# A one-element GpSimd add that reads the last prepared weight, ahead of GpSimd's first weight sums, and a newly searched list of steps, in a chunked-attention and gated feed-forward kernel

## The chip, the cores and the metric

The kernel runs on one core of a Trainium2 chip. The core's engines are TensorE (PE, matmuls; PEld is its weight load), VectorE (DVE), ScalarE (ACT), GpSimd (POOL) and SyncE (SP), which here only issues DMA transfers, one after the other in its program's order. Each engine works through its own instructions in order and waits on semaphores for what others make. The metric is the device time of one execution in microseconds, lower is better.

## The reference

Attention in chunks of 64 rows, without a sum across chunks, and after it a feed-forward layer on all tokens. Both matrices of the layer come as 64-bit floats (in the kernel: pairs of 32-bit words).

```python
scores = scale * q_c @ k_c.T          # q, k, v: (8, 8, 576, 64), chunks of 64
attn = exp(scores - max); attn /= (sum(attn) + 1e-9)
x = (attn @ v_c) laid out as (4608 tokens, 512)
h = x @ w_in                          # 512 x 2048
g = h * sigmoid(1.702 * h)
out = g @ w_out                       # 2048 x 512
```

## The kernel before

Tokens are worked in 9 blocks of 512 (four tiles of 128), and the 2048 hidden columns in 16 slices of 128. A group is one block with one slice; group g of the first three blocks is block g // 16, slice g % 16. For each group PE makes the slice of h (steps `h0_g` and `h_g`, six matmuls of 512 columns each; for groups 0 and 1 it is cut into halves, `hh_0_0`, `h_0_0`, `hh_0`, `h_0` and so on), ACT makes the activation and its rounded high part (`gh_g`), DVE the low part (`gl_g`), and PE adds into the four output tiles (`o_g_0` to `o_g_3`, three matmuls each). Every product is three matmuls on a high and a low part, so both weights and activations are split.

The weights of slice j are loaded by SP (`raw_j`: two transfers of 512 KB, w_in's and w_out's part, L365 and L370), and made into high and low parts by ACT (`wsc_j` L374, `wlow_j` L381, `wh_j` L410) and DVE (`wshift_j` L387, `wj_j` L394, `w_j` L413). DVE's three use one of three buffers called `wtmp`. PE needs `w_j` for `h0_j`.

Attention runs beside it: `q_u`, `k_u`, `v_u` are loads of the first four tiles; `rows0_4` and `rows1_4` load q and k of tiles 4 and 5 (two transfers of 256 KB each, L470). PE transposes those (`tp0_4`, `tp1_4`, L1259), ACT and DVE copy them (`tq0_4`, `tk0_4`), and `s_4` makes the scores. For later pairs of tiles (`s_6`, `s_8`, ...) DVE transposes (`tq0_8`, `tq1_8`, L1277; the attention weights by L1342, `et0_6` to `et_6`) and POOL divides (`n_6`, `n_8`, L1323).

From block 3 on pairs of blocks are multiplied with sums of blocks (seven products P1 to P7 in place of eight). For that POOL adds up parts of each pair of weight slices p: `pa0_p` and `pa_p` (L699, tile `whole`), then four sums (`psum_p`, L706 to L709, tile `sums`); these tiles too are `wtmp` buffers. ACT and DVE split them, SP writes them to a DRAM tile `seven` (`pout`, `pouts`), and later loads the pieces for each product (`ld0_s_p` to `ld6_s_p`, L807 and L809) into six buffers, used in turn.

`ORDER`, a list of 2,693 step names, sets in which order the steps are written to the program, and so the order on every engine and on SP's queue. `Plan.emit` asserts that each step's `need` names stand ahead of it in the list. A `need` is no wait on the chip by itself: the waits follow from the tiles that an instruction reads, writes or takes over.

```python
        plan.add(POOL, 1.3, rank, lambda: whole(0), need=[w0, f"w_{NF - 1}"], make=e("pa0"), take=["tmp"])
```

So in the list `pa0_p` stands behind `w_15`, while `whole(0)` reads only the weights of slice 2p and takes over one `wtmp` buffer.

Of the kernel before, what the change touches and what calls it, by code (L numbers as in the profile page):

```python
# [8 lines left out]
F32 = mybir.dt.float32  # L9
# [5 lines left out]
ALU = mybir.AluOpType  # L15
AX = mybir.AxisListType

PE, ACT, DVE, POOL, DMA = "pe", "act", "dve", "pool", "dma"
# [216 lines left out]
def tile_chunk_attention_ffn(  # L235
# [9 lines left out]
    nc = tc.nc  # L245
# [4 lines left out]
    P = 128  # L250
# [3 lines left out]
    NF = DF // P  # L254
# [1381 lines left out]
    def gelu_table():  # L1636
        z = const.tile([P, P], F32, tag="gelu", name="gelu")
        nc.scalar.activation(z[:, :1], ident[:, :1], AF.Gelu_apprx_sigmoid)
# [55 lines left out]
```

## Time and profile before

| | |
|---|---|
| median of 3 runs | 821.38 us (819.9 to 821.66) |
| the profiled execution | 821.13 us, of which span 819.4 us |
| PE busy | 807.3 us (99%), 6038 matmuls |
| DVE, ACT, POOL busy | 586.2, 383.5, 91.5 us |
| DMA | 131 MB, mean 160 GB/s |

The span runs from the first to the last instruction of the program; times in the rows below are microseconds from its start. Busy time of PE is the union of matmuls whose ends are modelled and overlap, so that a stretch can be fully busy by this count while successive matmuls start 0.23 us apart.

### The profile page before, as it was taken

How to read it: one execution, taken by the hardware profiler on the slowest of the kernel's cores; microseconds unless marked ns; L12 is line 12 of the kernel's file. 1: busy time of each engine (PE TensorE's matmuls, PEld its weight loads, DVE VectorE, ACT ScalarE, POOL GpSimd, SP SyncE). 2: the span in 40 equal slices, each digit the busy share in tenths (PEclk: the TensorE clock that was granted, in tenths of full speed). 3: DMA queues.
4: the chain of work that ended last, by engine and by line, in shares of the span. 5: the costliest groups of instructions: out<-in, count | busy, mean ns of one | idle time of the engine just before them, and what ended most of it. 6: DMA issues, size and time to landing. Idle time of an engine off the chain costs nothing.

```text
span 819.4 us, 15635 instructions
## 1 busy us (share of the span) xinstructions
PE 807.3 (99%) x6038; PEld 680.4 (83%) x6038; DVE 586.2 (72%) x865; ACT 383.5 (47%) x603; POOL 91.5 (11%) x82
## 2 busy tenths in 40 slices
PE   7899999999999999999999999999999999999998
PEld 6788878888888888888888888888888888889998
DVE  5788976356475879885698898776887454569852
ACT  5899824244355536423554352422565311267430
POOL 1000170000063661000001010000000000000000
PEclk9999999999999999999999999999999999999999
DMA  9998645353266677767666437686633047673433
GB/s 242 282 297 244 167 129 123 88 128 72 57 182 174 158 199 207 186 173 219 171 172 167 104 92 193 180 211 198 164 104 116 1 130 213 194 207 118 142 92 103
DMA packets 244010, 131.08 MB, mean 160 GB/s; under 512 B 187104, under 2 KB 211680, under 8 KB 243936
## 3 DMA queue, kind: packets, MB, share of 16 engines
q1 hardware_dynamic: 243936, 130.08, 58.6%
q8 instruction: 48, 0.79, 0.4%
q14 instruction: 26, 0.21, 0.1%
HBM read 97.52 MB, written 32.51 MB: 159 GB/s over the span
## 4 chain that ended last, share of the span: by engine, by line
PE 88%; DVE 4%; SPq 3%; ACT 2%; DMA 2%; issue 1%; DVEq 0%; ACTq 0%
PE po L1553 12%; PE po L1555 12%; PE po L1554 12%; PE hp L820 9%; PE hp L822 9%; PE hp L821 9%; PE hp L1515 4%; PE hp L1513 4%; PE hp L1514 4%; SPq L470 2%; PE s L1293 2%; PE x L1367 2%; DMA w<-seven 1%; DVE wtmp L394 1%; PE acc_X L1069 1%; PE acc_X L1068 1%
## 5 line engine op out<-in xcount | busy, mean ns | idle before, releaser
L1553 PE MATMUL po<-w,g_l 128*128 128x512 f32 x448 | 176.8, 395 | 0.6 <-DVE g_l L1543 0.5
L1555 PE MATMUL po<-w,g_h 128*128 128x512 f32 x448 | 174.5, 390 | 0.0
L1554 PE MATMUL po<-w,g_h 128*128 128x512 f32 x448 | 174.5, 389 | 0.0
L1553 PEld LDWEIGHTS po<-w,g_l 128*128 128x128 f32 x448 | 84.1, 188 | 20.1 <-DVE g_l L1543 1.9
L1555 PEld LDWEIGHTS po<-w,g_h 128*128 128x128 f32 x448 | 84.1, 188 | 17.7
L1554 PEld LDWEIGHTS po<-w,g_h 128*128 128x128 f32 x448 | 84.1, 188 | 16.8
L820 PE MATMUL hp<-w,w 128*128 128x512 f32 x224 | 87.6, 391 | 0.3 <-DMA w<-seven 0.2
L1342 DVE STREAM_TRANSPOSE eT<-e 32x512 f32<-32x512 f32 x120 | 84.2, 702 | 4.4 <-POOL e L1323 2.4
L822 PE MATMUL hp<-w,w 128*128 128x512 f32 x224 | 87.2, 389 | 0.0
L821 PE MATMUL hp<-w,w 128*128 128x512 f32 x224 | 87.1, 389 | 0.0
L1323 POOL TENSOR_TENSOR e<-e,r 128x1024 f32<-128x1024 f32 x16 | 31.2, 1953 | 437.8 <-DVE r L1320 365.0
L1513 PE MATMUL hp<-x_l,w 128*128 128x512 f32 x184 | 72.0, 391 | 0.0
L1515 PE MATMUL hp<-x_h,w 128*128 128x512 f32 x184 | 71.6, 389 | 0.0
L1514 PE MATMUL hp<-x_h,w 128*128 128x512 f32 x184 | 71.6, 389 | 0.0
L1543 DVE TENSOR_TENSOR g_l<-hp,g_h 128x512 fp32r<-128x512 f32 (+1 forms) x50 | 33.2, 664 | 51.9 <-ACT g_h L1538 51.8
L1537 ACT ACTIVATE hp<-hp 128x512 f32<-128x512 f32 (+1 forms) x50 | 28.4, 569 | 66.5 <-PE hp L1515 57.3
L820 PEld LDWEIGHTS hp<-w,w 128*128 128x128 f32 x224 | 42.0, 188 | 10.5 <-issue 1.1
L822 PEld LDWEIGHTS hp<-w,w 128*128 128x128 f32 x224 | 42.1, 188 | 8.8
L821 PEld LDWEIGHTS hp<-w,w 128*128 128x128 f32 x224 | 42.1, 188 | 8.6
L820 PE MATMUL hp<-w,pieces 128*128 128x512 f32 x112 | 43.8, 391 | 0.0
L822 PE MATMUL hp<-w,pieces 128*128 128x512 f32 x112 | 43.6, 389 | 0.0
L821 PE MATMUL hp<-w,pieces 128*128 128x512 f32 x112 | 43.6, 389 | 0.0
(237 smaller groups left out, 1558.6 us busy)
## 6 DMA issues: line engine op xcount, KB each, us to landing
w<-seven SPq DMA_DIRECT2D x112, 256.0 KB, 3.3
pieces<-seven SPq DMA_DIRECT2D x56, 256.0 KB, 3.4
seven<-w SPq DMA_DIRECT2D x24, 512.0 KB, 3.8
raw<-in_moe_w_in_dram SPq DMA_DIRECT2D x16, 512.0 KB, 5.9
raw<-in_moe_w_out_dram SPq DMA_DIRECT2D x16, 512.0 KB, 6.3
four<-four_w SPq DMA_DIRECT2D x32, 256.0 KB, 3.2
raw<-in_q_dram SPq DMA_DIRECT2D x208, 32.0 KB, 2.4
raw<-in_k_dram SPq DMA_DIRECT2D x208, 32.0 KB, 2.2
```

The costliest lines, as they stand in the source:

```text
L820: nc.tensor.matmul(hp, w[:, 0, c], xl[:, c], start=c == 0, stop=False)
L821: nc.tensor.matmul(hp, w[:, 0, c], xh[:, c], start=False, stop=False)
L822: nc.tensor.matmul(hp, w[:, 1, c], xh[:, c], start=False, stop=c == 1)
L1323: nc.gpsimd.tensor_tensor(st["e"], st["e"], bc(st["r"]), op=ALU.mult)
L1342: nc.vector.transpose(st["et"][po : po + 32, :, 32 * a : 32 * a + 32], st["e"][pi : pi + 32, :, 32 * b : 32 * b + 32],)
L1513: nc.tensor.matmul(hp, wh, xl, start=cc == 0, stop=False)
L1514: nc.tensor.matmul(hp, wh, xh, start=False, stop=False)
L1515: nc.tensor.matmul(hp, wl, xh, start=False, stop=cc == NCC - 1)
L1543: nc.vector.tensor_tensor(gl[:, c], hp, gh[:, c].bitcast(F32), op=ALU.subtract)
L1553: nc.tensor.matmul(po, gl[:, c], w[:, 0, :], start=first, stop=False)
L1554: nc.tensor.matmul(po, gh[:, c], w[:, 0, :], start=False, stop=False)
L1555: nc.tensor.matmul(po, gh[:, c], w[:, 1, :], start=False, stop=last)
```

## The change

A step `gate` is added on POOL: it adds one element of the last slice's low weight part to itself, into a tile that nobody reads. `pa0_p` now needs `gate` in the list in place of `w_15`; on POOL `gate` stands ahead of the first `pa0`. The list is another one from its first line on: it has the same names and `gate`.

```diff
-        plan.add(POOL, 1.3, rank, lambda: whole(0), need=[w0, f"w_{NF - 1}"], make=e("pa0"), take=["tmp"])
+        plan.add(POOL, 1.3, rank, lambda: whole(0), need=[w0, "gate"], make=e("pa0"), take=["tmp"])
...
+    def gate():
+        t = const.tile([P, 1], F32, tag="gate", name="gate")
+        w = wt[NF - 1][:, 1, 1, :1].bitcast(F32)
+        nc.gpsimd.tensor_tensor(t, w, w, op=ALU.add)
...
+    plan.add(POOL, 0.12, -80, gate, need=[f"w_{NF - 1}"], make="gate")
...
-    "o_85_0 tlo0_5 d5_1_3 thi1_5 tout0_5 P4_1_3 ld5_1_4 P1_1_4 d6_1_3 h_1_3_two ld3_1_4 tlo1_5 v0_30 gl_86 P2_1_4 "
...
+    "ld3_1_4 d3_1_3 tout_4 o_85_3 ta_5 o_84_1 tsum_5 o_85_0 gh_86 P3_1_3 d4_1_3 thi0_5 ld4_1_4 o_85_1 tlo0_5 P4_1_3 "
```

**The start, SP's queue** (`first_b` are the `v` loads, `rows_4` the loads `rows0_4` and `rows1_4`, `raw_j` the weights), before and then after, from `raw_1` on:

```order
L365 DMA raw_1_237<-in_moe_w_in_dram 128x4x128
L370 DMA raw_1_237<-in_moe_w_out_dram 128x512
L470 DMA rows_4_260<-in_q_dram 128x8x64
L470 DMA rows_4_260<-in_k_dram 128x8x64
L470 DMA first_b_3_245<-in_v_dram 128x8x64
L470 DMA first_b_2_314<-in_v_dram 128x8x64
L365 DMA raw_2_368<-in_moe_w_in_dram 128x4x128
L370 DMA raw_2_368<-in_moe_w_out_dram 128x512
L365 DMA raw_3_385<-in_moe_w_in_dram 128x4x128
```

```order
L365 DMA raw_1_234<-in_moe_w_in_dram 128x4x128
L370 DMA raw_1_234<-in_moe_w_out_dram 128x512
L470 DMA first_b_2_259<-in_v_dram 128x8x64
L470 DMA first_b_3_242<-in_v_dram 128x8x64
L365 DMA raw_2_312<-in_moe_w_in_dram 128x4x128
L370 DMA raw_2_312<-in_moe_w_out_dram 128x512
L470 DMA rows_4_356<-in_q_dram 128x8x64
L470 DMA rows_4_356<-in_k_dram 128x8x64
L365 DMA raw_3_391<-in_moe_w_in_dram 128x4x128
```

The two transfers of `rows0_4` moved from ahead of `raw_2` to behind it; what stands ahead of `raw_3` is the same.

**The start, PE** (`hp_0_1` is the second half of group 0, `hp_1_0` the first of group 1, `qkTp_4_0` is `tp0_4`, `po_0_1` is `o_0_1`), before and after, from the end of `o_0_0` on:

```order
L1555 MATMUL po_0_0_437<-w_0_289,g_h_0_375 128x512
L1553 MATMUL po_0_1_444<-w_0_289,g_l_0_376 128x512
...
L1526 MATMUL hp_0_1_454<-x_h_0_84,w_0_289 128x256 x4
L1526 MATMUL hp_1_0_461<-x_h_0_84,w_1_448 128x256 x4
L1528 MATMUL hp_0_1_454<-x_l_0_85,w_0_289 128x256
...
L1259 MATMUL qkTp_4_0_478<-ident_73,rows_4_260 128x128 x8
L1528 MATMUL hp_1_0_461<-x_l_0_85,w_1_448 128x256
```

```order
L1555 MATMUL po_0_0_435<-w_0_310,g_h_0_382 128x512
L1526 MATMUL hp_0_1_445<-x_h_0_84,w_0_310 128x256 x4
L1259 MATMUL qkTp_4_0_453<-ident_73,rows_4_356 128x128 x8
L1528 MATMUL hp_0_1_445<-x_l_0_85,w_0_310 128x256
...
L1526 MATMUL hp_1_0_479<-x_h_0_84,w_1_442 128x256 x4
L1553 MATMUL po_0_1_485<-w_0_310,g_l_0_383 128x512
...
L1528 MATMUL hp_1_0_479<-x_l_0_85,w_1_442 128x256
```

`tp0_4` moved ahead of `h_0`, `hh_1_0` and `o_0_1`; further on, two of the four `o_1` steps moved ahead of `h0_2`, and the steps up to the first `o_2` are the same set in both.

**The last weights, DVE** (around `g_l_12` and the last three `w_j`), before and after:

```order
L394 ISA wtmp_14_1150<-raw_14_911,wtmp_14_1150 128x2048
L413 TENSOR_TENSOR w_13_1174<-wtmp_13_1140,w_13_1174 128x2x512
L1342 STREAM_TRANSPOSE eT_6_1101<-e_6_1019 32x16x32 x2
L413 TENSOR_TENSOR w_14_1206<-wtmp_14_1150,w_14_1206 128x2x512
L387 TENSOR_SCALAR wtmp_15_1241<-raw_15_1067 128x1024
L1543 TENSOR_TENSOR g_l_12_1224<-hp_12_1186,g_h_12_1223 128x512
L394 ISA wtmp_15_1241<-raw_15_1067,wtmp_15_1241 128x2048
L1342 STREAM_TRANSPOSE eT_6_1101<-e_6_1019 32x16x32 x2
L1277 STREAM_TRANSPOSE qkT_8_1266<-raw_8_965 128x1024 x2
L1543 TENSOR_TENSOR g_l_13_1263<-hp_13_1227,g_h_13_1262 128x512
L413 TENSOR_TENSOR w_15_1253<-wtmp_15_1241,w_15_1253 128x2x512
```

```order
L413 TENSOR_TENSOR w_13_1182<-wtmp_13_1142,w_13_1182 128x2x512
L394 ISA wtmp_15_1184<-raw_15_928,wtmp_15_1184 128x2048
L1342 STREAM_TRANSPOSE eT_6_1128<-e_6_1016 32x16x32 x2
L413 TENSOR_TENSOR w_15_1216<-wtmp_15_1184,w_15_1216 128x2x512
L1543 TENSOR_TENSOR g_l_12_1223<-hp_12_1164,g_h_12_1222 128x512
L413 TENSOR_TENSOR w_14_1236<-wtmp_14_1112,w_14_1236 128x2x512
L1277 STREAM_TRANSPOSE qkT_8_1262<-raw_8_1002 128x1024
L1543 TENSOR_TENSOR g_l_13_1265<-hp_13_1207,g_h_13_1264 128x512
L1342 STREAM_TRANSPOSE eT_6_1128<-e_6_1016 32x16x32 x2
L1277 STREAM_TRANSPOSE qkT_8_1262<-raw_8_1002 128x1024
L1342 STREAM_TRANSPOSE eT_6_1128<-e_6_1016 32x16x32 x2
```

`w_15` came ahead of `g_l_12` and of `w_14`, `w_14` behind `g_l_12`; four of the eight transposes of tile pair 6 and one of pair 8's two now stand behind `g_l_13`.

**The last weights, POOL**, before and after, from `n_6` on:

```order
L1323 TENSOR_TENSOR e_6_1019<-e_6_1019,r_6_1061 128x1024
L699 TENSOR_TENSOR whole_2_1301<-w_4_664 128x512
L699 TENSOR_TENSOR whole_2_1301<-w_5_716 128x512
L699 TENSOR_TENSOR whole_0_1383<-w_0_289 128x512
L699 TENSOR_TENSOR whole_0_1383<-w_1_448 128x512
```

```order
L1323 TENSOR_TENSOR e_6_1016<-e_6_1016,r_6_1074 128x1024
L1639 TENSOR_TENSOR gate_1240<-w_15_1216 128x1
L699 TENSOR_TENSOR whole_2_1242<-w_4_660 128x512
L699 TENSOR_TENSOR whole_2_1242<-w_5_712 128x512
L699 TENSOR_TENSOR whole_0_1275<-w_0_310 128x512
L699 TENSOR_TENSOR whole_0_1275<-w_1_442 128x512
```

The gate stands between `n_6` and the first sums; behind them the order is `psum_2`, `psum_0`, one or both of pair 1, `n_8` in both.

## Rows read from the trace of the kernel before

**Rows 1.** The page's first lines: the span, and busy time, share and instructions of each engine.
```profile
span 819.4 us, 15635 instructions
PE 807.3 (99%) x6038; PEld 680.4 (83%) x6038; DVE 586.2 (72%) x865; ACT 383.5 (47%) x603; POOL 91.5 (11%) x82
```

**Rows 2.** Busy time of each engine in three stretches (start and end, length; then busy us and instructions; granted clock, DMA share, GB/s).
```profile
28.00:48.00 20.00, 18.35 (x163) 15.65 (x164) 17.03 (x24) 18.41 (x25) 0.00 (x0) 1.00 0.99 308
48.00:102.00 54.00, 53.87 (x359) 44.06 (x358) 48.75 (x53) 47.61 (x58) 3.81 (x2) 1.00 0.86 227
102.00:114.00 12.00, 11.49 (x50) 8.88 (x49) 11.85 (x13) 5.40 (x9) 6.45 (x4) 1.00 0.36 121
```

**Rows 3.** What PE waited for from 48 us to the end: us in total, times, longest.
```profile
PE po L1553 <- DVE g_l L1543: 0.5, 2, 0.3
PE hp L820 <- DMA w<-seven: 0.2, 1, 0.2
```

**Rows 4.** The chain that ended last, in order of time, from the transfer of `raw_2`'s second half to the first `o_2` (start, us, what).
```profile
23.82 6.60 DMA raw<-in_moe_w_out_dram
...
48.59 0.50 PE po L1553
```

**Rows 5.** ACT's instructions in order of time, 28 to 48 us: `wh_1`, `wsc_2`, `wsc_3`, `tq1_4`, the second half of `gh_2` (start, us; in brackets idle time before it and what ended it).
```profile
28.61 1.06 ACT L410 ACTIVATE w<-wtmp 128x1024 fp32r<-128x1024 f32 x1
30.50 1.17 ACT L374 ACTIVATE raw<-raw 128x1024 f32<-128x1024 f32 x1 [0.83 <-DMA raw<-in_moe_w_out_dram]
...
33.77 1.17 ACT L374 ACTIVATE raw<-raw 128x1024 f32<-128x1024 f32 x1
...
38.19 0.60 ACT L1266 ACTIVATE qkT<-qkTp 128x512 f32<-128x512 f32 x1 [0.57 <-DVE qkT L1269]
...
46.75 0.60 ACT L1538 ACTIVATE g_h<-hp 128x512 fp32r<-128x512 f32 x1
```

**Rows 6.** SP's issues of the k part of `rows0_4`, of `raw_3`'s second half and of the k part of `rows1_4`, and for each of them the us from issue to landing.
```profile
17.36 0.94 SPq L470 DMA_DIRECT2D rows<-in_k_dram  x1
24.84 0.50 SPq L370 DMA_DIRECT2D raw<-in_moe_w_out_dram  x1
26.16 2.70 SPq L470 DMA_DIRECT2D rows<-in_k_dram  x1
...
rows<-in_k_dram SPq DMA_DIRECT2D x1, 256.0 KB, 6.2
raw<-in_moe_w_out_dram SPq DMA_DIRECT2D x1, 512.0 KB, 8.8
rows<-in_k_dram SPq DMA_DIRECT2D x1, 256.0 KB, 9.0
```

**Rows 7.** PE's matmuls in order of time around the start of the attention of tiles 4 and 5: `o_0_1`, `hh_0` with `hh_1_0`, `tp0_4`, `h_1_0`, `hh_1`, `s_4`.
```profile
28.66 0.40 PE L1553 MATMUL po<-w,g_l 128*128 128x512 f32 x1
...
29.35 1.11 PE L1526 MATMUL hp<-x_h,w 128*128 128x256 f32 x8
...
31.25 1.03 PE L1259 MATMUL qkTp<-ident,rows 128*128 128x128 f32 x8
32.04 0.36 PE L1528 MATMUL hp<-x_l,w 128*128 128x256 f32 x1
...
33.91 0.73 PE L1526 MATMUL hp<-x_h,w 128*128 128x256 f32 x4 [0.68 <-DVE g_l L1543]
...
38.84 1.16 PE L1293 MATMUL s<-qkT 64*64 64x64 f32 x64 [0.97 <-ACT qkT L1266]
```

**Rows 8.** DVE's instructions in order of time: `w_6`, and `w_14`, `gl_12`, `wj_15`, `gl_13`.
```profile
61.73 1.23 DVE L413 TENSOR_TENSOR w<-wtmp,w 128x1024 fp32r<-128x1024 f32 x1
...
103.53 2.23 DVE L413 TENSOR_TENSOR w<-wtmp,w 128x1024 fp32r<-128x1024 f32 x1
...
106.28 0.68 DVE L1543 TENSOR_TENSOR g_l<-hp,g_h 128x512 fp32r<-128x512 f32 x1
106.88 1.70 DVE L394 CUSTOM_DVE_ANT_0 wtmp<-raw,wtmp 128x2048 uint16<-128x2048 uint16 x1
...
112.37 0.65 DVE L1543 TENSOR_TENSOR g_l<-hp,g_h 128x512 fp32r<-128x512 f32 x1
```

**Rows 9.** POOL's instructions in order of time: `pa0_2` with `pa_2`, `pa0_0` with `pa_0`, and `n_8`.
```profile
102.13 2.55 POOL L699 TENSOR_TENSOR whole<-w 128x512 f32<-128x512 f32 x2 [13.39 <-DVE w L413]
105.84 3.90 POOL L699 TENSOR_TENSOR whole<-w 128x512 f32<-128x512 f32 x2 [1.16 <-DVE w L413]
...
133.47 1.90 POOL L1323 TENSOR_TENSOR e<-e,r 128x1024 f32<-128x1024 f32 x1 [10.60 <-ACT hp L1537]
```

**Rows 10.** PE's matmuls in order of time: the first of `h0_6`, of `o_12_3` and of `o_13_3`.
```profile
63.23 0.39 PE L1513 MATMUL hp<-x_l,w 128*128 128x512 f32 x1
...
107.02 0.50 PE L1553 MATMUL po<-w,g_l 128*128 128x512 f32 x1 [0.19 <-DVE g_l L1543]
...
113.08 0.50 PE L1553 MATMUL po<-w,g_l 128*128 128x512 f32 x1 [0.32 <-DVE g_l L1543]
```

**Rows 11.** The chain that ended last, the transfers that it holds behind 500 us (start, us), and PE's first matmul of `P7_1_4`.
```profile
543.96 4.43 DMA w<-seven
...
711.13 5.00 DMA w<-seven
...
548.52 0.47 PE L820 MATMUL hp<-w,w 128*128 128x512 f32 x1 [0.20 <-DMA w<-seven]
```

340 rows, old and new, of the table ORDER are left out of this document.

## The prediction

> **What bounds the kernel now.** I read the page's first lines, then the busy times by stretch, then PE's waits, the chain that ended last, and at last the rows of each engine in the few places where PE stands still. PE is busy for 807.3 of 819.4 us [rows 1], so nothing but PE's gaps can be won back: 12.1 us in all. By stretch, PE lacks 1.65 us between 28 and 48 us, 0.13 in the 54 us behind that, and 0.51 between 102 and 114 us [rows 2]. From 48 us to the end only three waits show: two for a `g_l` of DVE (0.5 us) and one for a load of `seven` (0.2 us) [rows 3]. The rest lies in the first 28 us and in the last stores, where the list keeps its pace (below). The reader is to see that this change can win or lose in three places: the start up to the first `o_2` at 48.59 us, the end of the weights' preparation at 102 to 114 us, and the late loads. The sum is made against the profiled execution, 821.13 us, of which 819.4 are span; the median of the runs shown is 821.38. Within 0.2% (1.64 us) two versions of this kernel can hardly be told apart.
>
> **The gate itself.** One POOL instruction on one element: no row shows one, the nearest are POOL's other short instructions; it lies between nothing at all and one `whole` of 1.28 us (half of 2.55 [rows 9]). POOL is busy for 91.5 us of the span [rows 1], and what is queued behind it are the sums and then `n_8`. The sums started at 102.13 us and `n_8` at 133.47, after 10.6 us of idle time [rows 9]. The gate holds the sums until `w_15` is made, some 4 us later than before, and that idle time hides it. Without that cover `n_8`, and the `s_10` that PE makes behind it, would be late by 4 us. I take nothing.
>
> **The end of the weights (term B).** Before, POOL's first sums ran while DVE still prepared weights: `w_14` took 2.23 us and `wj_15` 1.70, where `w_6` took 1.23 [rows 8] and POOL's second pair 3.90 where the first took 2.55 [rows 9]. So the two engines hold each other up; DVE loses 1.00 us at `w_14` and, taking the same 1.23 for `wj_15`, 0.47 there. DVE is busy for 11.85 of the 12 us [rows 2], so this is passed on: PE waits 0.19 us for `gl_12` and 0.32 for `gl_13`, and each first matmul behind a wait takes 0.50 where others take 0.39 [rows 10]. That is 0.73 us to be won at most. In the changed list `gl_12` has `wj_15` and `w_15` ahead of it in place of `w_14` and two transposes of pair 6, 0.3 us less DVE work as I count it, and no sums beside it; it comes about 1.3 us earlier (0.3 + 1.0). But PE asks for it earlier too: one `o_11` step of 0.7 us (three matmuls, 28.66 to 29.35 [rows 7]) now stands behind `o_12_0`, and PE has a head start of 0.9 from term A. Against 107.02 less the lost 0.3, it asks at 105.1; DVE is done at 106.96 (106.28 + 0.68 [rows 8]) less 1.3, 105.7, and earlier by as much as DVE too has a head start. So PE waits 0 to 0.6 us; I take the middle. `gl_13` has three more transposes behind it instead of ahead of it and is out of PE's way. B = -0.73 + 0.3 = **-0.4**, with 0 and -0.73 as ends.
>
> Here a rule speaks against the change. With the gate, POOL's four `whole` start right behind `w_15`, and `w_14` follows on DVE only one `g_l` (0.68 us [rows 8]) later, so it meets them. The Trainium skill (SBUF — State Buffer, section Who interferes with whom) says that a DVE instruction with two SBUF inputs and a GpSimd instruction that reads SBUF exclude each other for the whole instruction. By it the contention is moved and not removed: `w_14` pays once more, and DVE wins back only 0.47 + 0.3 us over both weights. The trace agrees that they exclude each other (the 2.23 us above). The order of the queue keeps my sum from hanging on it: `w_14` now stands behind `gl_12`, and `gl_13` has about 4 us less DVE work ahead of it (three transposes gone, and both delays).
>
> **The start (term A).** The chain that ended last passes through `raw_2`'s landing at 30.42 us (23.82 + 6.60) to the first `o_2` at 48.59 [rows 4]. Before it, SP had put the two transfers of `rows0_4` into the queue ahead of `raw_2`; they landed by 23.6 us (17.36 + 6.2 [rows 6]), and PE needed them only at 31.25 [rows 7]. The change puts them behind `raw_2`. At 308 GB/s in this stretch [rows 2] their 512 KB are 1.7 us, so `raw_2` lands at 28.7, before ACT is done with `wh_1` at 29.67, and the 0.83 us that ACT waited for it go [rows 5]. Two things limit what comes of that.
>
> First ACT: `wsc_3` started at 33.77 [rows 5], with `raw_3` landed at 33.64 (24.84 + 8.8 [rows 6]), and what stands ahead of `raw_3` is the same set. If it lands as before, ACT starts `wsc_3` at 33.7 and needs 13.0 us to the end of `gh_2` (47.35 - 33.77 = 13.58 [rows 5], less the 0.57 that it waited before `tq1_4`, which goes because `tp1_4`'s rows had landed at 35.2 (26.16 + 9.0 [rows 6]) and the steps ahead of it come sooner). That is 46.7 instead of 47.35, so 0.65 us earlier; were `raw_3` sooner too, up to 1.4 (0.83 + 0.57).
>
> Second PE: `tp0_4` now stands ahead of `h_0`, `hh_1_0` and `o_0_1` and waits for `rows0_4`. From `tp0_4` at 31.25 to `o_2` at 48.59 were 17.34 us, less the two waits of 0.68 and 0.97 [rows 7] and 0.1 at each of three first matmuls; added to it are the three steps moved behind (28.66 to 31.25 [rows 7] less 0.5 for `hh_0`), 2.1: the first `o_2` comes 17.5 us after `rows0_4`'s landing. At the latest they land when the same set of loads had landed before, at 30.42: then `o_2` is at 47.9, 0.7 us earlier. Landing at 29.7 it is 1.4. Between 0.65 and 1.4, and nearer the first, A = **-0.9**.
>
> **The late loads (term C).** PE waited 0.20 us, and 0.1 in the first matmul, for the load of `P7_1_4` [rows 11]. In the old list this load stood on SP behind `ld5_1_4`, whose buffer comes free two products later; the new list has it right behind `ld2_1_4`. C = **-0.3**. The load issued at 711.13 us also took long, 5.00 us [rows 11], and the same two loads stand in the same order in both lists: nothing.
>
> All else is the same steps in other places, with PE full before and after. I put 0 on it, and 0.5 us either way for the range. Sum: -0.9 - 0.4 - 0.3 = -1.6, **819.5 us**; the best of all ends is -0.5 - 1.4 - 0.73 - 0.3, 818.2.
>
> **The rivals.** *The head start is eaten (820.5 us).* Past 48 us PE has little to spare: `w_6` was done at 62.96 (61.73 + 1.23 [rows 8]) and `h0_6` started at 63.23 [rows 10], 0.27 us. If ACT and DVE don't come 0.9 us sooner too, PE is back in step there and A shrinks to -0.3. B is then 0: DVE makes `gl_12` 1.3 us earlier, and I let waits of the new order at other tight weights take the 0.4. C stays, and the sum is -0.6. For it: DVE 48.75 and ACT 47.61 of 54 us busy [rows 2]. Against: DVE then idles 5.2 us of the 54.
>
> *Slower: `rows0_4` lands too late (822.9).* By the 17.5 us above, PE loses from a landing at 31.1 us on. For it: SP's issues block for long (2.70 us in [rows 6]), and a pair like it, `rows1_4`, took 9.0 us to land. Landing with `raw_3` at 33.64, the first `o_2` would be at 51.1, 2.5 us late; with B and C, +1.8. Against: the set of loads up to it is the one that had landed at 30.42.
>
> *The sums hold DVE (820.8).* If POOL's four `whole` (5.1 us) pass one behind the other ahead of `w_14`, `gl_13` comes 4.4 us later (5.1 less 0.68), and PE, whose `gl_13` had about 4 us to spare less the 0.9 of its head start, waits about 1.3 us: -1.6 + 1.3, 0.3 us below 821.13. By the skill's rule just cited the lock is given up after each instruction, and `w_14` would wait 1.3 us at most; the rows are with it, since `wj_15` at 106.88 got in between two `whole` [rows 8, 9].
>
> **The numbers.** Forecast 0.45, head start eaten 0.36, late rows 0.13, sums hold DVE 0.06. Faster by over 0.2% is the forecast: 0.45, since its 1.6 us lie at the bound and its upper end beyond. Within 0.2%: 0.42, the second and fourth. Slower: 0.13. The range is 818.0 (the best ends) to 821.9, which leaves out the worse half of the late rows. The forecast's own range is 818.2 to 820.0.
>
> **What the changed profile would show.** A: no wait of ACT before `wsc_2`, PE waiting before `tp0_4` for less than 1.3 us, the first `o_2` at 47.5 to 48.0. B: no POOL row between `n_6` and `w_15`'s end, DVE's `w_14` the only long one, PE idle for under 0.3 us where 0.51 stood. C: no wait for `seven` near 547 us. I am wrong if PE shows new waits of over 0.5 us past 48 us, or if `tp0_4` waits beyond 31 us.

## The result, and the profile after

The changed kernel takes 829.77 us (829.27 to 832.25) where the kernel before took 821.63 in the runs beside it: a ratio of 1.0106, 95% interval 1.0086 to 1.0126. It is slower by 8.1 us. The prediction said 819.5 us and gave a slower outcome 0.13.

The page of the changed kernel, its first lines (answering to [rows 1]):

```profile
span 828.2 us, 15624 instructions
PE 817.2 (99%) x6038; PEld 680.7 (82%) x6038; DVE 585.4 (71%) x865; ACT 381.6 (46%) x603; POOL 91.9 (11%) x83
```

Busy time by stretch (the columns of [rows 2]: from and to, length, then PE, PEld, DVE, ACT, POOL busy with their instructions, granted clock, DMA share, GB/s):

```profile
28.00:48.00 20.00, 18.60 (x164) 15.66 (x163) 16.95 (x23) 18.43 (x25) 0.48 (x1) 1.00 1.03 309
48.00:102.00 54.00, 54.00 (x355) 43.56 (x354) 46.89 (x53) 47.42 (x56) 3.57 (x2) 1.00 0.83 237
102.00:114.00 12.00, 12.00 (x53) 9.74 (x52) 11.23 (x13) 5.14 (x8) 9.02 (x9) 1.00 0.65 182
...
560.00:700.00 140.00, 140.00 (x901) 113.54 (x900) 89.96 (x142) 56.41 (x96) 4.06 (x2) 1.00 0.42 124
```

Read the first three against [rows 2]: PE's gaps are smaller than before in each, and none is left from 48 us on; the waits for `g_l` and for `seven` of [rows 3] are gone. By the prediction's own method the kernel should be faster. But PE is busy for 817.2 us where it was 807.3, with the same 6038 matmuls at a granted clock of 1.00, the upper of PE's two levels, in these stretches. The last row shows how: 140 us in which PE never stops, and 901 matmuls fit in. Before, the same stretch held 912:

```profile
560.00:700.00 140.00, 140.00 (x912) 115.43 (x911) 90.71 (x141) 54.12 (x91) 4.06 (x2) 1.00 0.45 131
```

So nothing waits, and each matmul takes longer. Groups of PE and PEld by line (busy us, mean ns of one, idle time before), of the kernel before:

```profile
L1553 PE MATMUL po<-w,g_l 128*128 128x512 f32 x448 | 176.8, 395 | 0.6 <-DVE g_l L1543 0.5
L1555 PE MATMUL po<-w,g_h 128*128 128x512 f32 x448 | 174.5, 390 | 0.0
...
L1554 PEld LDWEIGHTS po<-w,g_h 128*128 128x128 f32 x448 | 84.1, 188 | 16.8
...
L1514 PE MATMUL hp<-x_h,w 128*128 128x512 f32 x184 | 71.6, 389 | 0.0
...
L822 PE MATMUL hp<-w,pieces 128*128 128x512 f32 x112 | 43.6, 389 | 0.0
```

and of the changed one:

```profile
L1553 PE MATMUL po<-w,g_l 128*128 128x512 f32 x448 | 178.9, 399 | 0.0
L1555 PE MATMUL po<-w,g_h 128*128 128x512 f32 x448 | 177.1, 395 | 0.0
...
L1554 PEld LDWEIGHTS po<-w,g_h 128*128 128x128 f32 x448 | 84.2, 188 | 19.5
...
L1514 PE MATMUL hp<-x_h,w 128*128 128x512 f32 x184 | 71.8, 390 | 0.0
...
L822 PE MATMUL hp<-w,pieces 128*128 128x512 f32 x112 | 44.3, 396 | 0.0
```

The o_* matmuls (they stream `w` and have `g_h` or `g_l` as weights) and the products whose weights are `pieces` are 4 to 7 ns longer; `h_*` (streams x, weights `w`) is hardly changed, and the weight load shows 188 ns in both. From the records of the trace I took the time from one matmul's start to the next where both are of one kind, waits (over 250 ns) left out: o_* went from 227.1 to 232.7 ns on average, `pieces` from 227.0 to 233.1, `h_*` from 226.9 to 228.7, the acc_* matmuls of 256 columns from 120.0 to 119.3.

What differs for these operands is where they lie. The new tile `gate` is taken from the pool `const`, ahead of many tiles; with its 4 bytes it takes 32 in each partition. In the compiled programs `g_h` starts at byte 203,392 before and 203,424 after, `pieces` at a multiple of 64 before and 32 past one after, while `w` (34,432) and x stay where they were.

Executions of one kernel can differ by 2.4 us with how late PE's clock rises at the start (last section), and the medians below mix them.

### The profile page after: what moved, and what is told of

Same layout as the page of the kernel before. It is cut to its first block, busy times and chain, and to the rows that moved or that the text cites. A ratio compares the mean times of both kernels' runs of the same rounds, so it can differ in the third digit from the quotient of the medians.

```text
span 828.2 us, 15624 instructions
## 1 busy us (share of the span) xinstructions
PE 817.2 (99%) x6038; PEld 680.7 (82%) x6038; DVE 585.4 (71%) x865; ACT 381.6 (46%) x603; POOL 91.9 (11%) x83
## 4 chain that ended last, share of the span: by engine, by line
PE 95%; SPq 3%; DMA 1%; ACT 0%; DVE 0%; issue 0%; ACTq 0%
PE po L1553 13%; PE po L1555 12%; PE po L1554 12%; PE hp L822 9%; PE hp L820 9%; PE hp L821 9%; PE hp L1515 5%; PE hp L1513 5%; PE hp L1514 5%; PE s L1293 2%; PE x L1367 2%; SPq L470 2%; SPq L365 1%; PE acc_X L1069 1%; PE acc_Y L1069 1%; PE acc_X L1067 1%
## 5 line engine op out<-in xcount | busy, mean ns | idle before, releaser
L1553 PE MATMUL po<-w,g_l 128*128 128x512 f32 x448 | 178.9, 399 | 0.0
L1555 PE MATMUL po<-w,g_h 128*128 128x512 f32 x448 | 177.1, 395 | 0.0
L1554 PE MATMUL po<-w,g_h 128*128 128x512 f32 x448 | 176.8, 395 | 0.0
L1553 PEld LDWEIGHTS po<-w,g_l 128*128 128x128 f32 x448 | 84.1, 188 | 20.4 <-DVE g_l L1543 0.4
L835 ACT ACTIVATE d<-hp 128x512 f32<-128x512 f32 x24 | 14.3, 595 | 69.0 <-PE hp L822 62.7
L822 PE MATMUL hp<-w,pieces 128*128 128x512 f32 x112 | 44.3, 396 | 0.0
L821 PE MATMUL hp<-w,pieces 128*128 128x512 f32 x112 | 44.3, 395 | 0.0
```

Source lines behind the costliest of these rows:

```text
L821: nc.tensor.matmul(hp, w[:, 0, c], xh[:, c], start=False, stop=False)
L822: nc.tensor.matmul(hp, w[:, 1, c], xh[:, c], start=False, stop=c == 1)
L1553: nc.tensor.matmul(po, gl[:, c], w[:, 0, :], start=first, stop=False)
L1554: nc.tensor.matmul(po, gh[:, c], w[:, 0, :], start=False, stop=False)
L1555: nc.tensor.matmul(po, gh[:, c], w[:, 1, :], start=False, stop=last)
```

## The experiments

The distance is that of the start of `g_h` from that of `w` in bytes, modulo 256 (`pieces` has the same one from what its products stream). Spacing is the mean start to start as above.

| kernel | list | distance | o_* ns | `pieces` ns | `h_*` ns | median us | ratio to before (95%) |
|---|---|---|---|---|---|---|---|
| before | old | 0 | 227.1 | 227.0 | 226.9 | 820.6 to 821.6 | |
| changed | new | 32 | 232.7 | 233.1 | 228.7 | 829.77 | 1.0106 [1.0086, 1.0126] |
| old32 | old | 32 | 232.8 | 233.0 | 228.4 | 831.69 | 1.0130 [1.0116, 1.0144] |
| oldw32 | old | 224 (-32) | 233.3 | 233.3 | 227.7 | 831.62 | 1.0129 [1.0115, 1.0142] |
| oldall32 | old | 0 | 227.2 | 226.9 | 227.0 | 822.46 | 1.0018 [1.0007, 1.0029] |
| oldall128 | old | 0 | 227.1 | 226.9 | 226.9 | 820.62 | 0.9994 [0.9984, 1.0003] |
| new64 | new | 64 | 233.4 | 233.4 | 228.8 | 831.15 | 1.0117 [1.0101, 1.0133] |
| new128 | new | 128 | 232.8 | 232.9 | 228.2 | 830.24 | 1.0104 [1.0083, 1.0126] |
| new192 | new | 192 | 229.4 | 229.3 | 227.1 | 821.68 | 1.0009 [0.9996, 1.0021] |
| new256 | new | 0 | 227.1 | 226.7 | 226.8 | 818.19 | 0.9961 [0.9946, 0.9976] |
| newtop | new | 0 | 227.0 | 226.7 | 226.9 | 818.14 | 0.9960 [0.9947, 0.9973] |
| nogate | new | 0 | 227.1 | 226.7 | 226.8 | 818.11 | 0.9966 [0.9953, 0.9978] |

**Address or list?** First I put the shift alone into the kernel before:

```diff
-        z = const.tile([P, P], F32, tag="gelu", name="gelu")
+        z = const.tile([P, P + 8], F32, tag="gelu", name="gelu")
```

> The kernel before, list and instructions untouched; only its gelu tile is 32 bytes wider, so that g_h, g_l, pieces and all that lies behind start 32 bytes past a multiple of 64, as in the changed kernel. If the address makes the matmuls slow (theory): the o_* matmuls and the products whose weights are pieces go from 227 to about 232 to 233 ns from start to start, and the time from 821.6 to about 831.5 us (830 to 833). If the new list or the gate makes them slow (rival): 821.6 us, 227 ns.

Measured: 831.69 us. No instruction and no order differ from the kernel before, only the places of the tiles behind `gelu`, and the loss is there whole (L1553, and the stretch from 560 us):

```profile
L1553 PE MATMUL po<-w,g_l 128*128 128x512 f32 x448 | 179.0, 399 | 0.3 <-DVE g_l L1543 0.3
```
```profile
560.00:700.00 140.00, 140.00 (x901) 113.40 (x900) 91.99 (x145) 54.50 (x93) 4.07 (x2) 1.00 0.44 128
```

The other way round, the list without the gate and its tile:

```diff
-        plan.add(POOL, 1.3, rank, lambda: whole(0), need=[w0, "gate"], make=e("pa0"), take=["tmp"])
+        plan.add(POOL, 1.3, rank, lambda: whole(0), need=[w0, f"w_{NF - 1}"], make=e("pa0"), take=["tmp"])
...
-    plan.add(POOL, 0.12, -80, gate, need=[f"w_{NF - 1}"], make="gate")
```

> The changed kernel's list without the gate: no instruction and no tile for it, the first sums held by nothing on w_15; all PE operands at multiples of 64 by that. Theory (address): 227 ns, and of the prediction's terms the start (-0.9) and the late load (-0.3) without the end of the weights (-0.4): about 820.2 us (819.3 to 821). Rival, the new list makes PE slow: 829.8. Rival, the gate instruction: 820.2 too, but then new64 stays at 829.8.

Measured: 818.11 us against 821.25, 3.1 less: the new list is a gain, and more than the 1.2 us that I expected of it.

**An address, or a distance between two?** I first took it for alignment to 64 bytes.

```diff
-        t = const.tile([P, 1], F32, tag="gate", name="gate")
+        t = const.tile([P, 16], F32, tag="gate", name="gate")
...
-        nc.gpsimd.tensor_tensor(t, w, w, op=ALU.add)
+        nc.gpsimd.tensor_tensor(t[:, :1], w, w, op=ALU.add)
```

> The changed kernel, its gate tile 64 bytes wide in place of 4, so that the tiles behind it start at multiples of 64 again (but not of 128, as they did before the change). Theory, with 64 bytes as what counts: all 512-column matmuls at 227 ns again, about 819.5 us, the forecast of the prediction (818.5 to 820.5). With 128 bytes as what counts: near 829.8. Rival, list or gate: 829.8 us.

Measured: 831.15, as slow as with 4 bytes. That theory fell. Beside it ran the kernel that moves `w` and x and leaves `g_h` and `pieces`:

```diff
-    ident = const.tile([P, P], F32, tag="ident", name="ident")
+    ident = const.tile([P, P + 8], F32, tag="ident", name="ident")[:, :P]
...
-        z = const.tile([P, P], F32, tag="gelu", name="gelu")
+        z = const.tile([P, P - 8], F32, tag="gelu", name="gelu")
```

> The kernel before, with 32 bytes added ahead of x_h, x_l and the w tiles and 32 bytes taken from the gelu tile behind them: now w, x and the attention's tiles lie 32 past a multiple of 64, while g_h, g_l and pieces are where they were. It parts the two operands. If it is the stationary operand (the weights that PE loads): the h_* matmuls and the products whose weights are w slow by some 6 ns (552 + 672 of them, about 7 us: 828 to 830 us), the o_* ones, which stream w and load g, stay at 227. If it is the streamed operand: o_*, h_* and products slow alike, 1344 + 552 + 1008 by 5 to 6 ns, 836 to 839 us. If neither (list): 821.6.

Measured: 831.62, and neither case: o_* is slow though its weights lie as before, `h_*` is not though both its operands moved.

```profile
L1554 PE MATMUL po<-w,g_h 128*128 128x512 f32 x448 | 177.0, 395 | 0.0
...
L1514 PE MATMUL hp<-x_h,w 128*128 128x512 f32 x184 | 71.6, 389 | 0.0
```

In `h_*` the two operands moved together, in o_* one of them did. So the new theory was the distance between what a matmul streams and the weights that PE loads, and the test of it moves everything (only the first of the two edits above):

> The kernel before with 32 bytes added ahead of all tiles but the first (ident): x, w, g_h, g_l, pieces all move by 32 bytes together, so every address differs from before while the distance between the operand that a matmul streams and the weights that PE loads stays as it was. Theory now (the distance between the two operands counts, modulo some power of two): 227 ns between matmuls and 821.3 us (820 to 822.3). Rival (an address of its own counts, of g or of w): 232 to 233 ns and about 831 us.

Measured: 227.2 ns, with `w` and `g_h` both 32 past a multiple of 64. The distance decides. The time of 822.46 us is 1.4 above before, and the spacing has no part in it: the profiled execution, at 824.89 us the slowest of the ten, shows waits of PE for `g_l` of 1.9 us in all and for loads of `seven` of 1.6, the two kinds of [rows 3], and one of 1.3 for `x_l`. Whether the addresses make these was asked with 128 bytes in place of 32:

> The kernel before with 128 bytes added ahead of all tiles but ident: like oldall32, distances unchanged. 227 ns between matmuls by the theory. It asks whether the 1.4 us that oldall32 was above before come from its addresses being 32 past a multiple of 64 (then 821.0 here) or from any shift (822.4). Rival (128 bytes on every address collide as 128 on the distance do): 830.

Measured: 820.62 against 820.61. A shift of all tiles by 128 bytes costs nothing; whether what oldall32 lost comes from its 32 bytes stays open.

**Which distances?** The gate's tile 128, 192 and 256 bytes wide (`[P, 32]`, `[P, 48]`, `[P, 64]`):

> The changed kernel with the gate tile 128 bytes wide: g_h, g_l, pieces stand 128 bytes from where they would stand without it, w and x where they were. If the distance counts modulo 128 bytes: 227 ns, about 818 us. If modulo 256 or 512: 231 to 234 ns for o_* and pieces, about 829 to 831 us. The first theory (a multiple of 64 or 128 is enough for each address) expects 818 too.

> The changed kernel with the gate tile 192 bytes wide. If the distance between streamed operand and weights has to be a multiple of 256 bytes: slow as with 4, 64 and 128 bytes, 231 to 236 ns for o_* and pieces, 829 to 831 us. Rival (only distances below 192 collide): 227 ns, 818.1 us.

> The same with the gate tile 256 bytes wide. Modulo 256: 227 ns, about 818 us. Modulo 512 or more: 231 to 234 ns, about 829 to 831 us.

Measured: 128 is slow, 256 is not, and 192 lies between, at 229.4 ns. In the programs every distance of these matmuls in the kernel before is 0 modulo 512 bytes too. So 0 and 256 were fast and 32 to 192 slow, and so was 32 the other way round (oldw32); nothing between 256 and 480 modulo 512 was tried, and that the period is 256 rests on these two values. Of new128 and of new256, the same 140 us:

```profile
560.00:700.00 140.00, 140.00 (x902) 114.01 (x902) 90.80 (x143) 56.37 (x96) 4.07 (x2) 1.00 0.42 126
```
```profile
560.00:700.00 140.00, 140.00 (x914) 115.73 (x913) 90.78 (x140) 55.77 (x94) 4.07 (x2) 1.00 0.43 128
```

**The change without the shift.** The same list and gate, the gate's tile in a pool of its own behind all others:

```diff
+    top = ctx.enter_context(tc.tile_pool(name="top", bufs=1))
...
-        t = const.tile([P, 1], F32, tag="gate", name="gate")
+        t = top.tile([P, 1], F32, tag="gate", name="gate")
```

> The changed kernel, list and gate instruction as they are, with the gate's tile at the top of SBUF behind all other tiles, so that none of them moves. Theory (only the moved addresses made it slow): 227 ns and about 817.7 us: the list without a gate gave 818.1, and by the prediction's second term the gate takes the sums off DVE at w_14 (-0.4). Rival (the gate's wait or the list costs something as well): above 819.

Measured: 818.14 us, 11.6 below the changed kernel, from which it differs in that place alone. It beats both kernels, as nogate does; between the two nothing can be told. Added up over PE's records of the two traces, the changed kernel spends 7.3 us more from start to start in o_*, 2.2 in the `pieces` products, 1.4 in `h_*`, 1.2 in the other products, 0.4 in the rest and 0.7 less in acc_*: 11.8, which is the whole difference of the spans (828.2 and 816.4).

**The prediction's terms alone.** The gate in the old list, its tile at the top:

```diff
-    ... o_13_2 pa0_2 pout1_0 ...
+    ... o_13_2 gate pa0_2 pout1_0 ...
```

> The kernel before with its own list, plus the gate alone: the one-element add stands behind w_15, ahead of the first sums, and its tile lies at the top of SBUF so that nothing moves. The prediction's second term alone: no sums beside w_14 and wj_15 (1.2 us each again), 0.4 us gained (0 to 0.73): about 820.6 us. Rival (the gate gains nothing, as the new list with and without it suggests, 818.14 and 818.11): 821.0 us.

Measured: 819.84 against 820.61, ratio 0.9990 [0.9980, 0.9999]. POOL's first rows, DVE's `w_14` and `wj_15`, and 102 to 114 us:

```profile
113.61 0.19 POOL L1641 TENSOR_TENSOR gate<-w 128x1 f32<-128x1 f32 x1 [24.00 <-DVE w L415]
113.76 4.99 POOL L701 TENSOR_TENSOR whole<-w 128x512 f32<-128x512 f32 x4
```
```profile
104.41 1.23 DVE L415 TENSOR_TENSOR w<-wtmp,w 128x1024 fp32r<-128x1024 f32 x1
...
106.76 1.21 DVE L396 CUSTOM_DVE_ANT_0 wtmp<-raw,wtmp 128x2048 uint16<-128x2048 uint16 x1
```
```profile
102.00:114.00 12.00, 12.00 (x55) 9.94 (x54) 11.51 (x14) 6.30 (x9) 0.39 (x2) 1.00 0.44 135
```

Against [rows 8] `w_14` is back from 2.23 to 1.23 us and `wj_15` from 1.70 to 1.21, and PE's 0.51 us of gaps in [rows 2] are gone. At the old list the gate does what it says, for its 0.19 us.

By the count of matmuls, this profile's PE gains 1.13 us against before's between 104 and 116 us, more than the 0.73 that the prediction took as the most.

The place of `rows0_4`, ahead of `raw_2` again (but behind the `v` loads, where the kernel before has it ahead of them):

```diff
-    ... wh_0 raw_2 xp_0 ... hh_0_0 xl_0 rows0_4 z_2 ...
+    ... wh_0 rows0_4 raw_2 xp_0 ... hh_0_0 xl_0 z_2 ...
```

> The changed kernel with the gate's tile at the top of SBUF, and with rows0_4 put back ahead of raw_2, nothing else. The prediction's first term (the start is gained by that place): ACT waits 0.8 us before wsc_2 again and the first o_2 is about 1 us later, 818.1 + 0.9 = 819.0 us. Rival (the gain at the start comes from the other steps that moved): 818.1 us.

Measured: 818.57 in the median, ratio 0.9980 [0.9969, 0.9991]. Seven of its twelve times are 817.8 to 818.8 and show no loss against newtop's 817.7 to 818.5; the other five are 820.4 to 820.9, and the one of them that was profiled has a cause of its own (last section). The rival's 818.1 fits.

## Why the prediction was wrong

**The step that failed** is "All else is the same steps in other places, with PE full before and after. I put 0 on it, and 0.5 us either way for the range." It took PE's pace as a constant. That term is 11.8 us instead, the changed kernel's span over newtop's, and it is the shift of `g_h`, `g_l` and `pieces` against what is streamed with them. Without it the change gains, as forecast and more: 818.14 us (newtop) where the sum gave 819.5. Nothing in the trace of before could size the shift, but its possibility was in the diff: a new tile in the pool `const`, in a kernel where PE is busy for 99%. Of the gate I costed the instruction and its queue, and not its tile. The signs that I named for being wrong, new waits past 48 us and a late `tp0_4`, are absent from the changed kernel's profile (`tp0_4` starts at 29.31); there was none for a slower matmul.

**The gate itself**: right. It takes 0.19 us. In newtop `n_8` starts at 131.63, earlier than in [rows 9], behind 14.37 us of idle time.

**Term A (-0.9)**: near in size by luck; its reason failed. In newtop the first `o_2` starts at 47.75 us where it was 48.59 [rows 4], -0.84; in the changed kernel at 48.32, later than the 47.5 to 48.0 that the prediction named. There ACT no longer waits before `wsc_2`, but `raw_3`, issued at 27.37 where it was 24.84 [rows 6], lands at 33.81, and ACT waits for it (the two `wsc` rows of the changed kernel, then those of newtop, answering to [rows 5]):

```profile
29.35 1.19 ACT L374 ACTIVATE raw<-raw 128x1024 f32<-128x1024 f32 x1
...
33.90 1.14 ACT L374 ACTIVATE raw<-raw 128x1024 f32<-128x1024 f32 x1 [1.12 <-DMA raw<-in_moe_w_out_dram]
```
```profile
29.74 1.20 ACT L375 ACTIVATE raw<-raw 128x1024 f32<-128x1024 f32 x1
...
33.07 1.15 ACT L375 ACTIVATE raw<-raw 128x1024 f32<-128x1024 f32 x1
```

But `rows0_4` ahead of `raw_2` cost nothing in newrows. There `raw_2` was issued at 23.83, as in [rows 4], with the same two transfers ahead of it, and landed 4.9 us later where it took 6.60. And the old list comes as early with its own queue: in oldall32's profile ACT does not wait before `wsc_2` and the first `o_2` starts at 47.65; in old32 and oldall128 ACT waits 0.22 and 0.19 us and `o_2` starts at 48.10 and 48.15. So most of the 0.83 us wait belonged to the one execution that I sized the term by, and how much the new list gains at the start, if anything, is not shown.

**Term B (-0.4)**: the gain is there (PE is full from 102 to 114 us in the changed kernel, newtop and nogate), the reason holds for the old list only, and 0.73 us was too little as the most. I counted the idle time and 0.1 us for each first matmul. From start to start, in before's rows around the two waits of [rows 10], two intervals of 0.227 us took 0.91 and 1.05:

```profile
106.44 0.39 PE L1555 MATMUL po<-w,g_h 128*128 128x512 f32 x1
...
107.35 0.39 PE L1554 MATMUL po<-w,g_h 128*128 128x512 f32 x1
...
112.37 0.39 PE L1555 MATMUL po<-w,g_h 128*128 128x512 f32 x1
...
113.42 0.40 PE L1554 MATMUL po<-w,g_h 128*128 128x512 f32 x1
```

So the two waits cost 0.46 and 0.59 us, 1.05 in all, and newtop and oldgate win that back (1.13 each by the count of matmuls from 104 to 116 us). In the changed kernel the four `whole` meet `w_14`, as the prediction said:

```profile
104.88 0.19 POOL L1639 TENSOR_TENSOR gate<-w 128x1 f32<-128x1 f32 x1 [14.00 <-DVE w L413]
105.02 6.04 POOL L699 TENSOR_TENSOR whole<-w 128x512 f32<-128x512 f32 x4
```
```profile
105.32 2.08 DVE L413 TENSOR_TENSOR w<-wtmp,w 128x1024 fp32r<-128x1024 f32 x1
```

The Trainium skill (SBUF — State Buffer, section Who interferes with whom) says that a DVE instruction with two SBUF inputs contends with a GpSimd instruction that reads SBUF; the trace agrees, `w_14` taking 2.08 us here and 1.23 in oldgate, where no sums ran beside it. In nogate both late weights pay, 2.02 and 1.93 us, and PE stays full all the same: the new order keeps `gl_12` and `gl_13` out of their way, and the gate adds nothing to it.

**Term C (-0.3)**: right, and too small for the same reason. PE is busy for all of 540 to 560 and of 700 to 730 us in the changed kernel, where it lacked 0.20 and 0.14 in the trace of before; for the second I had put nothing. Counted by matmuls, newtop wins 0.47 us at the first and 0.42 at the second. Together the list gains 3.1 us in the medians (nogate) where A and C make 1.2: by the same count nogate, without the gate, wins 0.94 us between 104 and 116 us, the place of B, and 0.46 and 0.41 at the two loads; the rest is 1.17 us at the start, which differs with the execution, and some tenths elsewhere. The old list's waits for `g_l` and `seven` behind 48 us differ too: 3.5 us in oldall32's profile, 0.7 in [rows 3], 0.4 in oldgate's, none in any profile of the new list.

**The rivals**: none came. The head start was not eaten (counted by matmuls, nogate was 1.08 us ahead of before at about 40 us and 1.17 at 76), `rows0_4` landed at 29.19 us, ahead of the 31.1 from which PE would have lost, and `gl_13` waited for ACT (0.40 us) and not for the sums.

## What to carry to other kernels

A new tile, however small, moves those allocated behind it. In a kernel that PE bounds, compare the start addresses of what matmuls stream and of what they load as weights before and after an edit, keep the distance that was fast (here a multiple of 256 bytes), and put small helper tiles behind all others. Compare also the count of matmuls in a stretch in which PE never waits: it shows a change of pace that waits and busy shares don't.

## What the runs showed of the hardware

The pace of 512-column matmuls depends on the distance between two operands: 227 ns at 0 modulo 256 bytes, 232.7 to 233.4 at 32, 64, 128 and 224, 229.4 at 192 (0 and 256 were both fast; 224 is 32 the other way). It is passed on to neighbours: in old32 the last `h_*` matmul ahead of an o_* takes 235 ns, while `h_*` matmuls with six of their kind ahead of them and one behind take 226.9; in new64 that last one takes 227, and the first three behind an o_* are slow, 229 to 233. The Trainium skill (SBUF — State Buffer, section Who interferes with whom) lists two independent read ports of PE, one for the streamed operand and one for the weights; by that these distances should not matter, and the measurement decides that here they do. What in SBUF or PE the two meet in was not shown, nor whether other types do the same. The acc_* matmuls of 256 columns go the other way: those of `pieces` with `w` and of `w` with `c_h` (a high part like `g_h`) take 120.0 ns in before, at distance 0, and 114.2 and 113.0 in new192, at 192, while those of `w` with `w`, at 0 in both, take 120.0 and 119.8.

The second one is a late clock. In some executions PE's 64-column matmuls run late from 8 to 14 us, in newrows (first row) as against newtop (second), and PE is 2.4 us late from 40 us on and 2.2 at the end:

```profile
9.96 3.58 PE L531 MATMUL s<-first_a 64*64 64x64 f32 x64
```
```profile
8.70 2.09 PE L530 MATMUL s<-first_a 64*64 64x64 f32 x64
```

The views give the granted clock as 1.00 from 8 to 14 us in both, but the records of the clock in the traces begin only at 13.29 us in newrows and at 6.56 in newtop, with 1.00. PE's pace changes there: 128-column matmuls start 213 to 214 ns apart ahead of that point and 109 behind it, in both. So ahead of it PE ran at the lower of its two levels. The records begin at 12.3 to 13.5 us in new64, new128 and new192 too, at 10.6 in oldw32, at 9.4 in oldgate, and at 4.6 to 6.7 in the other profiles. Ahead of the rise PE ran 14 matmuls of `warm` and then its first transposes in both; what delays the rise was not tried.
